# Layer 2 of a fused attention + two-MLP kernel as one Strassen level on 768-token superblocks

## Chip, cores and metric

One core of one Trainium2 chip. The time is the device time of the launch in microseconds (us), median of three runs. The core has five engines: TensorE (PE, with its weight loads shown as PEld), VectorE (DVE), ScalarE (ACT), GpSimd (POOL) and SyncE (SP, which issues the DMAs). TensorE multiplies a stationary 128x128 block of weights with a moving operand of up to 512 columns and adds the result into a bank of PSUM; all other data lies in SBUF.

## What is computed

```python
def _moe_ref(x, w_in, w_out):            # layer 1
    h = x @ w_in
    g = h * (1.0 / (1.0 + np.exp(-1.702 * h)))
    return (g @ w_out).astype(np.float32)

def _moe2_ref(x, w_in, w_out):           # layer 2
    h = x @ w_in
    r = np.maximum(h, 0.0)
    g = r * r
    return (g @ w_out).astype(np.float32)

# reference: x = attention(q, k, v) as 2304 tokens x 512; moe2(moe(x))
# w_in is 512 x 2048, w_out 2048 x 512, both arrive as float64
```

The attention is banded (32 keys, plain or dilated by 4), 4 batches x 8 heads x 576 x 64.

## The kernel before

Every product is made in three passes: an operand is split into a high part (a cast to fp32r) and a low part (value minus high part), and high x high, high x low and low x high are summed in PSUM.

Layer 1 goes over five blocks of tokens (512, 512, 256, 512, 512 columns, `BLOCKS1`, with the attention of later tokens worked in between), layer 2 over five more (`BLOCKS2`, the same sizes). `step` (L631) is one of the 16 slices f of 128 hidden features for one block: 12 matmuls "hidden" (four slices k of the inputs, three passes, L616 to L618) into a bank of PSUM named h, the activation (layer 1: `tanh` on ACT, L639, and `times_h` on DVE, L642; layer 2: `relu` on ACT, L649, and `square` on DVE, L652), the split of the result g into gh (`copy`, L251 on ACT or L253 on DVE) and gl (`minus`, L262, DVE), and 12 matmuls "project" (L683 to L685) into the four banks o, which sum over all 16 f. So a block is 16 x 24 = 384 matmuls of its number of columns. The last step of the last block is cut into two halves of 256 columns. The results go out through ost; layer 1's to a DRAM tensor x2d, from which layer 2 reads its input back.

All weights stay in SBUF: 32 places w{f}_{part} of 2 x 2 KB a partition. `weights` (L302) fills one: a load of the float64 words (L312), the top half word to f16 (`top`, ACT or DVE), `join` into a float32 (L327, DVE), high part, low part. Layer 2's weights go into the same places while layer 1's last block runs through them.

The order of the instructions on each engine is fixed beforehand by `Schedule.emit` (L132): tasks with costs, due times (`want`), predecessors and buffers are laid out one by one, and each engine then runs its list strictly in that order. SP does so too: a DMA that waits for a buffer holds up all DMAs behind it. `AHEAD` lets the hidden matmuls of a step run 24 matmuls (48 in layer 1's last block and in layer 2) ahead of their due time.

## Time and profile before

| | |
|---|---|
| median of 3 runs (lowest, highest) | 875.66 us (875.12, 877.23) |
| profiled execution: span, first to last instruction | 873.0 us |
| median over span (what lies around it) | 2.66 us |
| busy: PE, DVE, ACT, POOL | 863.3, 455.4, 368.1, 15.8 us |
| weight loads (PEld, beside PE) | 720.6 us |
| moved by DMA, mean rate | 64.99 MB, 74 GB/s |
| granted TensorE clock, mean | 1.000 |

No own time is given for the profiled execution beyond its span; the three runs lie 2.1 to 4.2 us above that span. Busy time is the time in which an engine has an instruction in work; matmuls overlap each other and their ends are modelled, so what one matmul costs is read from the distance of two starts, not from its duration.

### The profile page before, as it was taken

How to read it: one execution, taken by the hardware profiler on the slowest of the kernel's cores; microseconds unless marked ns; L12 is line 12 of the kernel's file. 1: busy time of each engine (PE TensorE's matmuls, PEld its weight loads, DVE VectorE, ACT ScalarE, POOL GpSimd, SP SyncE). 2: the span in 40 equal slices, each digit the busy share in tenths (PEclk: the TensorE clock that was granted, in tenths of full speed). 3: DMA queues.
4: the chain of work that ended last, by engine and by line, in shares of the span. 5: the costliest groups of instructions: out<-in, count | busy, mean ns of one | idle time of the engine just before them, and what ended most of it. 6: DMA issues, size and time to landing. Idle time of an engine off the chain costs nothing.

```text
span 873.0 us, 12807 instructions
## 1 busy us (share of the span) xinstructions
PE 863.3 (99%) x4758; PEld 720.6 (83%) x4758; DVE 455.4 (52%) x1254; ACT 368.1 (42%) x976; POOL 15.8 (2%) x25
## 2 busy tenths in 40 slices
PE   8999999999999999999999999999999999999997
PEld 6887778777899888888888888888889988888886
DVE  5998995466699843358788222322222232222222
ACT  7999995444455521134645222322222222222222
POOL 3300000000000000000000000000000000000000
PEclk9999999999999999999999999999999999999999
DMA  7655662111232020027554100100010000001001
GB/s 245 209 185 203 211 215 93 37 36 38 72 93 64 28 91 1 1 64 259 193 184 156 61 1 1 36 25 1 1 48 2 1 25 1 1 0 50 1 1 48
DMA packets 27534, 64.99 MB, mean 74 GB/s; under 512 B 3056, under 2 KB 9200, under 8 KB 27472
## 3 DMA queue, kind: packets, MB, share of 16 engines
q1 hardware_dynamic: 27472, 64.18, 22.1%
q8 instruction: 37, 0.61, 0.3%
q14 instruction: 25, 0.20, 0.1%
HBM read 54.73 MB, written 9.44 MB: 74 GB/s over the span
## 4 chain that ended last, share of the span: by engine, by line
PE 97%; ACT 1%; DVE 1%; DMA 0%; issue 0%; SPq 0%; DVEq 0%
PE h L616 16%; PE o L683 15%; PE h L618 15%; PE h L617 15%; PE o L684 15%; PE o L685 15%; PE s L467 3%; PE pv L568 2%; ACT sm L490 1%; DMA qk<-in_qkv 0%; PE tp L549 0%; PE warm L745 0%; DVE x L584 0%; ACT pt L251 0%; DVE pt L253 0%
## 5 line engine op out<-in xcount | busy, mean ns | idle before, releaser
L683 PE MATMUL o<-gh,wh 128*128 128x512 f32 (+3 forms) x648 | 238.5, 368 | 0.0
L685 PE MATMUL o<-gl,wh 128*128 128x512 f32 (+3 forms) x648 | 236.5, 365 | 0.0
L684 PE MATMUL o<-gh,wl 128*128 128x512 f32 (+3 forms) x648 | 236.5, 365 | 0.0
L616 PE MATMUL h<-x,wh 128*128 128x512 f32 (+3 forms) x520 | 190.9, 367 | 0.0
L618 PE MATMUL h<-x,wl 128*128 128x512 f32 (+3 forms) x520 | 187.3, 360 | 0.0
L617 PE MATMUL h<-x,wh 128*128 128x512 f32 (+3 forms) x520 | 187.1, 360 | 0.0
L262 DVE TENSOR_TENSOR gl<-g,gh 128x512 fp32r<-128x512 f32 (+3 forms) x163 | 102.1, 627 | 126.5 <-ACT gh L251 122.6
L683 PEld LDWEIGHTS o<-gh,wh 128*128 128x128 f32 x648 | 122.1, 188 | 21.6
L685 PEld LDWEIGHTS o<-gl,wh 128*128 128x128 f32 x648 | 122.2, 189 | 19.8
L684 PEld LDWEIGHTS o<-gh,wl 128*128 128x128 f32 x648 | 122.2, 189 | 19.3
L652 DVE TENSOR_TENSOR g<-g 128x512 f32<-128x512 f32 (+1 forms) x81 | 51.2, 632 | 157.9 <-ACT g L649 157.8
L251 ACT CAST gh<-g 128x512 fp32r<-128x512 f32 (+3 forms) x117 | 68.4, 585 | 133.8 <-PE o L684 126.1
L649 ACT ACTIVATE g<-h 128x512 f32<-128x512 f32 (+1 forms) x81 | 44.5, 550 | 165.4 <-PE h L618 165.4
L616 PEld LDWEIGHTS h<-x,wh 128*128 128x128 f32 x520 | 98.1, 189 | 17.9
L618 PEld LDWEIGHTS h<-x,wl 128*128 128x128 f32 x520 | 98.1, 189 | 15.1
L617 PEld LDWEIGHTS h<-x,wh 128*128 128x128 f32 x520 | 98.2, 189 | 14.0
L639 ACT ACTIVATE g<-h 128x512 f32<-128x512 f32 (+3 forms) x82 | 44.4, 543 | 112.6 <-PE h L618 112.1
L490 ACT ACTIVATE sm<-sm,st 96x128 f32<-96x128 f32 x180 | 70.4, 395 | 40.4 <-DVE st L483 40.3
L642 DVE SCALAR_TENSOR_TENSOR g<-g,h 128x512 f32<-128x512 f32 (+3 forms) x82 | 50.4, 616 | 67.5 <-ACT g L639 67.0
L534 DVE STREAM_TRANSPOSE pt<-sm 32x192 f32<-32x192 f32 x144 | 53.1, 369 | 5.4 <-ACT sm L257 3.5
L618 PE MATMUL h<-xx,wl 128*128 128x512 f32 (+1 forms) x132 | 50.5, 383 | 0.0
L617 PE MATMUL h<-xx,wh 128*128 128x512 f32 (+1 forms) x132 | 50.5, 383 | 0.0
(66 smaller groups left out, 695.6 us busy)
## 6 DMA issues: line engine op xcount, KB each, us to landing
raw<-in_w SPq DMA_DIRECT2D x64, 511.8 KB, 3.3
qk<-in_qkv SPq DMA_DIRECT2D x32, 304.0 KB, 3.0
v<-in_qkv SPq DMA_DIRECT2D x32, 192.0 KB, 2.5
x2d<-ost SPq DMA_DIRECT2D x16, 256.0 KB, 2.1
raw<-x2d SPq DMA_DIRECT2D x16, 256.0 KB, 2.8
out_T<-ost SPq DMA_DIRECT2D x14, 256.0 KB, 2.0
x2d<-ost SPq DMA_DIRECT2D x4, 128.0 KB, 1.7
raw<-x2d SPq DMA_DIRECT2D x4, 128.0 KB, 2.2
```

The costliest lines, as they stand in the source:

```text
L251: A.copy(out, in_)
L262: by_name[e].tensor_tensor(out=out, in0=a, in1=b, op=ALU.subtract)
L490: A.activation(out=m["sm", j][:, i], in_=m["sm", j][:, i], func=AF.Exp, bias=m["st"][:, 0, j, i:i + 1], scale=-1.0, accum_out=m["st"][:, 1 ...
L534: V.transpose(out=pt[32 * e:32 * e + 32, :, :, 32 * a:32 * a + 32].rearrange("p j i q -> p (j i) q"), in_=m["sm"][32 * a:32 * a + 32, :, : ...
L616: T.matmul(out, w_hi[:, ks], x[:, 0, k, a:z], start=(k == 0), stop=False)
L617: T.matmul(out, w_hi[:, ks], x[:, 1, k, a:z], start=False, stop=False)
L618: T.matmul(out, w_lo[:, ks], x[:, 0, k, a:z], start=False, stop=(k == KD - 1))
L642: V.scalar_tensor_tensor(out=g(), in0=g(), scalar=1.0, in1=h(), op0=ALU.add, op1=ALU.mult)
L652: by_name[e].tensor_tensor(out=g(), in0=g(), in1=g(), op=ALU.mult)
L683: T.matmul(out, w_hi[:, ds_], m["gh"], start=(f == 0 and a == 0 or extra), stop=False)
L684: T.matmul(out, w_lo[:, ds_], m["gh"], start=False, stop=False)
L685: T.matmul(out, w_hi[:, ds_], m["gl"], start=False, stop=(f == KF - 1))
```

## The change

Layer 2 is done on three superblocks of 768 tokens. Both products are cut 2 x 2 and made from seven products of quarters in place of eight (Winograd's form, `PRODUCTS`). A matmul has now 384 columns (`HN`).

- `prepare` makes the seven combinations of the weights for one pair of f slices, each as a high and a low part, from two loads; 16 such calls (8 of w_out, 8 of w_in) are due 10 us apart (`PREP`) from layer 1's block 3 on. Their results are written to DRAM, wo_s and wi_s; six of w_in also stay in the places wp1 to wp6.
- `stream` loads the combined weights back, two DMAs a place, for each superblock anew: 8 places of w_in and 7 of w_out.
- `x_prep` loads 768 tokens of x2d and makes and splits the seven combinations of the input.
- `hidden2` does the first product for one pair of f slices: seven products of 6 matmuls, with the sums of Winograd's form done by DVE and ACT from PSUM into the planes gq, then relu and square (two ACT instructions or one of DVE, on 768 elements), then the differences T1 and T3.
- `output2` does the second product: seven products of four chunks of 12 matmuls; every chunk's operand (768 elements) is split into gh and gl right before.

The 32 places of the weights become eight of 16 KB; they also hold the planes and the streamed weights. Outside of layer 2, one of three buffers for v is given up, and the masks are loaded by two DMAs.

```diff
-MORE_LATE = 1.0
-W2_GAP = 4.0
+GB_US = 340.0
+PREP = 10.0
...
-BLOCKS2 = [512, 512, 256, 512, 512]
+SB = 768
+HN = SB // 2
+NSB = NT // SB
+NPR = KF // 2
+A11, A12, A21, A22, S1, S2, S4 = range(7)
+S3 = A21
+PRODUCTS = (
+    (A11, "B11"), (S4, "B22"), (S1, "T1"), (S2, "T2"), (A12, "B21"), (S3, "T3"), (A22, "T4"),
+)
+PLANE = {"B11": 0, "B12": 1, "B21": 2, "B22": 3, "T1": 4, "T2": 3, "T3": 1, "T4": 2}
+G_SLOTS = (7, 2, 3, 4)
+S_SLOTS = (5, 6, 0, 1)
+LAG = 3
+KEPT = 6
+FIRST_SLOTS = (1, 2, 3, 4, 5, 6, 0, 1)
+X_EARLY = 20.0
...
     x2d = dram.tile([KD, P, NT], F32, name="x2d")
+    wi_s = dram.tile([NPR, P, 2 * 7 * 256], F32, name="wi_s")
+    wo_s = dram.tile([7, P, 2, NPR, 256], F32, name="wo_s")
...
-    for f in range(KF):
-        for part in range(2):
-            places[f"w{f}_{part}"] = 1
+    for j in range(NPR):
+        places[f"wp{j}"] = 1
...
+    def prepare(n, part, j, want, cls):
+        m = {}
+        odd = n % 2
+        raw_bs = [buffer("x1")] if odd else [buffer("raw"), buffer("raw")]
+        w_cls = ("rh", "rl") if cls == "r" else (cls, cls)
+        w_bs = [buffer("rh"), buffer("rl")] if cls == "r" else [buffer(cls)] * 2
+        gate = x_users["x1"] if odd else raws_free
...
+        joins = []
+        for i in range(2):
+            mi = {}
...
+            t = task(
+                "dma", moved(P * 4096), want - 10, lambda i=i: load_weights(raw(i), 1, 2 * j + i, part), gate, [raw_bs[i % len(raw_bs)]],
+                since=begin[3] - 12,
+            )
+            t = task(*TOP, want - 5, lambda e, i=i, mi=mi: raw_top(e, raw(i), mi), [t], [raw_bs[i % len(raw_bs)], c_b], True)
+            joins.append(task("dve", JOIN, want - 5, lambda i=i, mi=mi: raw_join(raw(i), mi), [t], [raw_bs[i % len(raw_bs)], c_b], True))
+        def combine(out, a, b, op):
+            V.tensor_tensor(out=at(out), in0=at(a), in1=at(b), op=op)
+        def combined(out, a, b, op, after):
+            return task("dve", pairs(256)[1][0], want - 4, lambda: combine(out, a, b, op), after, raw_bs, True)
+        t1 = combined(S1, A21, A22, ALU.add, joins)
+        t3 = combined(S3, A11, A21, ALU.subtract, [t1])
+        t2 = combined(S2, S1, A11, ALU.subtract, [t1])
+        t4 = combined(S4, A12, S2, ALU.subtract, [t2])
...
+        his, los = [], []
+        for i, odd_word, after in ((0, 0, [t3]), (1, 0, [t3]), (0, 1, [t2]), (1, 1, [t4])):
+            width = 256 if (i, odd_word) == (1, 1) else 512
...
+            hi = task(*copies(width), want - 2, high, after + slot_users[w_cls[0]], [raw_bs[i % len(raw_bs)], w_bs[0]], True)
+            los.append(task(*pairs(width), want - 2, low, [hi] + slot_users[w_cls[1]], [raw_bs[i % len(raw_bs)]] + w_bs[0:1 + (cls == "r")], True))
+            his.append(hi)
...
+        def store(hl):
+            src = wt(hl).bitcast(F32)
+            if part == 0:
+                nc.sync.dma_start(wi_s[j][:, hl * 1792:(hl + 1) * 1792], src.rearrange("p i c -> p (i c)"))
+            else:
+                nc.sync.dma_start(wo_s[:, :, hl, j].rearrange("i p c -> p i c"), src)
+        stores = [
+            task("dma", moved(P * 7168), want - 1, lambda hl=hl: store(hl), (his, los)[hl], [w_bs[hl]]) for hl in range(2)
+        ]
...
+    def stream(cls, want, src, shape, after):
...
+        def load(hl):
+            if "w" not in m:
+                m["w"] = slot(cls, shape, F32R, "ws")
+            nc.sync.dma_start(m["w"][:, hl].bitcast(F32).rearrange("p i c -> p (i c)"), src[:, hl * n:(hl + 1) * n])
+        ts = [
+            task("dma", moved(P * n * 4), want, lambda hl=hl: load(hl), after + slot_users[cls], [w_b]) for hl in range(2)
+        ]
+        return (lambda: m["w"]), w_b, ts
...
+    OPS = {"rh": ("B11",), "rl": ("B22",), "r": ("T1",), "x0": ("T2", "B21"), "x1": ("T3",), "raw": ("T4",)}
+    def x_prep(s, want, cls):
...
+        loads = [
+            task(
+                "dma", moved(P * SB * 4), want - 8,
+                lambda k=k: nc.sync.dma_start(stage()[:, k], x2d[k, :, c0:c0 + SB]),
+                [stored[i, k] for i in need] + slot_users[cls], [st_b],
+            )
+            for k in range(KD)
+        ]
...
+        def split(op, after):
+            b = bufs_of(op)
+            hi = task(*copies(n768), want, lambda e: copy(e, place(op, 0), quarter(op)), after + op_users[home[op][0]], [st_b, b[0]], True)
+            lo = task(*pairs(n768), want, lambda e: minus(e, place(op, 1), quarter(op), place(op, 0)), [hi], [st_b] + b, True)
...
+        split("B11", [loads[0], loads[1]])
+        split("B22", [loads[2], loads[3]])
+        t1 = combine("T1", "B12", "B11", done["B11"])
+        split("T1", [t1])
+        t3 = combine("T3", "B22", "B12", [t1] + loads[2:])
+        t2 = combine("T2", "B22", "T1", [t3] + done["B22"])
+        split("T2", [t2])
+        split("B21", [loads[2], loads[3]])
+        split("T3", [t3])
+        t4 = combine("T4", "B21", "T2", [t2] + done["B21"])
+        split("T4", [t4])
...
+    def hidden2(s, j, x, w, last, gate, planes):
...
+        def product(n, key, cls, first, bufs, after, lag):
+            a, op = PRODUCTS[n]
...
+                for k in range(2):
+                    ks = slice(k * P, (k + 1) * P)
+                    hi, lo = place(op, 0)[:, k], place(op, 1)[:, k]
+                    T.matmul(out, wt[:, 0, a, ks], hi, start=(first and k == 0), stop=False, skip_group_check=True)
+                    T.matmul(out, wt[:, 0, a, ks], lo, start=False, stop=False, skip_group_check=True)
+                    T.matmul(out, wt[:, 1, a, ks], hi, start=False, stop=(k == 1), skip_group_check=True)
+            return task("pe", 6 * mm(HN), at + (n + lag) * unit, run, w_ready + x_done2[op] + after, bufs + [w_b] + bufs_of(op))
...
+        p_1 = product(0, "X", "s", True, [x_b], last, 0)
+        p_3 = product(1, "Y3", "o", True, [y3], [p_1], 0)
+        p_5 = product(2, "Z", "h", True, [z_b], [p_3], 0)
+        e1 = kept("p1", "X", [p_1] + gate, [x_b, p1_b], when(-LAG))
+        e3 = kept("p3", "Y3", [p_3], [y3, p3_b], when(1 - LAG))
+        p_6 = product(3, "X", "s", False, [x_b], [p_5, e1], LAG)
+        u2 = summed(None, "p3", "X", [p_6, e3], [x_b, p3_b], when(3))
+        c12 = summed(1, "p3", "Z", [p_5, u2], [z_b, p3_b, g_b], when(4))
+        p_2 = product(4, "Y2", "o", True, [y2], [p_6], LAG)
+        c11 = summed(0, "p1", "Y2", [p_2, e1], [y2, p1_b, g_b], when(4))
+        p_7 = product(5, "X", "s", False, [x_b], [p_2, u2], LAG)
+        e7 = kept("u3", "X", [p_7], [x_b, u3_b], when(5))
+        c22 = summed(3, "u3", "Z", [p_5, e7], [z_b, u3_b, g_b], when(6))
+        p_4 = product(6, "Y4", "o", True, [y4], [p_7], LAG)
+        c21 = summed(2, "u3", "Y4", [p_4, e7], [y4, u3_b, g_b], when(6))
...
+        ways = ("act", "dve"), (2 * (0.19 + n768 / 1536), pairs(n768)[1][0])
...
+            t1 = task(*pairs(n768), when(12), lambda e: diff(4, 1, 0), [a01, b01], [g_b], True)
+            t3 = task(*pairs(n768), when(13), lambda e: diff(1, 3, 1), [t1, a23, b23], [g_b], True)
...
+    def output2(s, planes, next_slot):
...
+        for n, (a, op) in enumerate(PRODUCTS):
+            want = at + n * LB
+            cls = next_slot()
+            wt, w_b, loaded = stream(cls, want - 30, wo_s[a].rearrange("p h j c -> p (h j c)"), [P, 2, NPR, 256], wo_stored)
...
+            for q in range(NPR // 2):
...
+                def high(e, mm_=mm_, third=third, pl=pl, plane=plane):
+                    pool, tag, k = (wst, "raw", RAW_BUFS) if third else (gpool, "gh", 2)
+                    mm_["h"] = pool.tile([P, 2, HN], F32R, tag=tag, bufs=k, name="gh")
+                    copy(e, mm_["h"], pl["tile"]()[:, plane])
+                def low(e, mm_=mm_, pl=pl, plane=plane):
+                    mm_["l"] = gpool.tile([P, 2, HN], F32R, tag="gl", name="gl")
+                    minus(e, mm_["l"], pl["tile"]()[:, plane], mm_["h"])
+                hi = task(*copies(n768), wq - 3, high, pl[op] + (raws_free if third else []) + split_last[0:1], [pl["b"], gh_b], True)
+                lo = task(*pairs(n768), wq - 3, low, [hi] + split_last[1:2], [pl["b"], gh_b, gl_b], True)
+                split_last[:] = [hi, lo]
+                if op == "B22":
+                    pl["T2"] = [task(*pairs(n768), wq + LB, lambda e, pl=pl: pl["diff"](3, 3, 4), [hi, lo] + pl["T1"] + pl["T3"], [pl["b"]], True)]
...
+                def project(q=q, mm_=mm_, wt=wt, key=key, first=first, b_cls=b_cls):
+                    w = wt()
+                    for d in range(2):
+                        if first and q == 0:
+                            m[key, d] = bank(b_cls, key)
+                        out, ds_ = m[key, d][:, 0:HN], slice(d * P, (d + 1) * P)
+                        for jj in range(2):
+                            j = 2 * q + jj
+                            hi, lo = mm_["h"][:, jj], mm_["l"][:, jj]
+                            T.matmul(out, w[:, 0, j, ds_], hi, start=(first and j == 0), stop=False, skip_group_check=True)
+                            T.matmul(out, w[:, 1, j, ds_], hi, start=False, stop=False, skip_group_check=True)
+                            T.matmul(out, w[:, 0, j, ds_], lo, start=False, stop=(j == NPR - 1), skip_group_check=True)
+                t = task("pe", LB / 4, wq, project, loaded + [hi, lo] + bank_after.get(n, []) + before, bs + [w_b, gh_b, gl_b])
...
+    want, n = begin[3], 0
+    for part, j in [(1, j) for j in range(NPR)] + [(0, j) for j in range(KEPT, NPR)]:
+        prepare(n, part, j, want, "r")
+        want, n = want + PREP, n + 1
+    r_stores = wo_stored + [t for ts in wi_stored.values() for t in ts]
+    first_w = {}
+    for j in range(KEPT):
+        first_w[j] = prepare(n, 0, j, max(want, begin[4] + (2 * j + 6) * step_len(512)), f"wp{j + 1}")
+        want, n = want + PREP, n + 1
...
+    x = x_prep(0, T2 - X_EARLY, "wp0")
...
+    for s in range(NSB):
+        planes, last = {}, []
...
+                w = stream(cls, T2 + s * LSB + j * LA - 30, wi_s[j], [P, 2, 7, 256], wi_stored[j])
+            last, by_op = hidden2(s, j, x, w, last, all_prepared if s == 0 else [], planes)
+            slot_users[cls] = list(by_op.values())
+        op_users = {cls: [by_op[op] for op in ops] for cls, ops in OPS.items()}
+        op_users["rh"] = op_users["rl"] = op_users["r"] = op_users["rh"] + op_users["rl"] + op_users["r"]
+        if s + 1 < NSB:
+            x = x_prep(s + 1, T2 + s * LSB + NPR * LA + 2 * LB, "x2")
+        output2(s, planes, next_slot)
...
```

In the order of instructions three places show what moves. First VectorE in layer 1's block 3 (g, gh, gl: a step's activation and split; raw, c: weights in the making; wt: a combination's high or low part), before:

```order
L642 SCALAR_TENSOR_TENSOR g<-g,h 128x512
L253 CAST gh<-g 128x512
L262 TENSOR_TENSOR gl<-g,gh 128x512
L262 TENSOR_TENSOR xx<-raw_3774,xx 128x512
L642 SCALAR_TENSOR_TENSOR g<-g,h 128x512
```

and with the change:

```order
L338 SCALAR_TENSOR_TENSOR raw<-raw,c 128x512
L277 TENSOR_TENSOR wt<-raw,wt 128x2x256 x2
L277 TENSOR_TENSOR wt<-raw,wt 128x512
L277 TENSOR_TENSOR wt<-raw,wt 128x256
L680 SCALAR_TENSOR_TENSOR g<-g,h 128x512
L338 SCALAR_TENSOR_TENSOR raw<-raw,c 128x512
L887 TENSOR_TENSOR raw<-raw 128x256
L277 TENSOR_TENSOR gl<-g,gh 128x512
L887 TENSOR_TENSOR raw<-raw 128x256 x2
L268 CAST wt<-raw 128x2x256
```

Between a step's g and its gl there now stand instructions of the weights. Second VectorE in layer 2, in the second product of the first superblock (gq: planes and their differences; p: sums of the output; X, Z: PSUM):

```order
L1136 TENSOR_TENSOR gq<-gq 128x768
L277 TENSOR_TENSOR gl<-gq,gh 128x768
L1170 TENSOR_TENSOR p_5770<-p_5770,X 128x384
L1170 TENSOR_TENSOR p_5775<-p_5775,X 128x384
L1170 TENSOR_TENSOR p_5770<-p_5770,Z 128x384
L1170 TENSOR_TENSOR p_5775<-p_5775,Z 128x384
L277 TENSOR_TENSOR gl<-gq,gh 128x768
```

One gl stands there for every chunk of TensorE, with differences and sums between. Third SyncE over the end of the first superblock and the start of the second (ws: streamed weights; xs: input):

```order
L958 DMA ws<-wo_s 128x2048 x12
L988 DMA xs<-x2d 128x768 x4
L958 DMA ws<-wo_s 128x2048 x2
L958 DMA ws<-wi_s 128x1792 x2
L1176 DMA out_T<-p_5770 128x384
L1176 DMA out_T<-p_5775 128x384
```

Before, layer 2's part of this queue held the loads of x2d and the stores of the result alone.

## Rows read from the trace of the kernel before

**Rows 1.** The page, busy time: engine, us, share, instructions
```profile
PE 863.3 (99%) x4758; PEld 720.6 (83%) x4758; DVE 455.4 (52%) x1254; ACT 368.1 (42%) x976; POOL 15.8 (2%) x25
```
**Rows 2.** The page, 40 slices: PE, and the granted clock in tenths
```profile
PE   8999999999999999999999999999999999999997
...
PEclk9999999999999999999999999999999999999999
```
**Rows 3.** The page, the chain of work that ended last, by engine
```profile
PE 97%; ACT 1%; DVE 1%; DMA 0%; issue 0%; SPq 0%; DVEq 0%
```
**Rows 4.** Timeline of PE, layer 2, 512 columns: start us, us
```profile
600.04 0.39 PE L617 MATMUL h<-x,wh 128*128 128x512 f32 x1
...
603.89 0.39 PE L616 MATMUL h<-x,wh 128*128 128x512 f32 x1
```
**Rows 5.** Timeline of PE, layer 2, 256 columns
```profile
654.75 0.28 PE L684 MATMUL o<-gh,wl 128*128 128x256 f32 x1
...
659.91 0.28 PE L618 MATMUL h<-x,wl 128*128 128x256 f32 x1
```
**Rows 6.** Instructions that read wl, weight loads: ns min/median/max
```profile
L618 PEld LDWEIGHTS h<-x,wl x520: 187/188/192, 30.2 to 772.0; 128*128 128x128 f32 x174
```
**Rows 7.** Stretches: length, busy PE, PEld, DVE, ACT, POOL, clock, DMA share, GB/s
```profile
390.00:412.00 22.00, 22.00 (x99) 18.18 (x98) 18.84 (x35) 11.95 (x20) 0.00 (x0) 1.00 0.77 253
...
455.00:477.00 22.00, 22.00 (x99) 18.22 (x98) 19.83 (x35) 12.29 (x22) 0.00 (x0) 1.00 0.46 157
```
**Rows 8.** Groups by line and form, DVE: count, busy us, mean ns
```profile
L262 DVE TENSOR_TENSOR gl<-g,gh 128x512 fp32r<-128x512 f32 x125 | 86.1, 689 | 112.3 <-ACT gh L251 109.7 <-PE pv L568 0.7
...
L327 DVE SCALAR_TENSOR_TENSOR raw<-raw,c 128x512 uint32<-128x512 uint32 x64 | 43.5, 686 | 2.1 <-ACT c L251 1.8
...
L262 DVE TENSOR_TENSOR gl<-g,gh 128x256 fp32r<-128x256 f32 x34 | 14.4, 423 | 14.2 <-ACT gh L251 12.9 <-PE o L684 0.7
L253 DVE CAST gh<-g 128x512 fp32r<-128x512 f32 x28 | 12.0, 427 | 7.0 <-PE o L684 5.1
```
**Rows 9.** Timeline of DVE, layer 1's last block: start us, us
```profile
440.67 0.43 DVE L253 CAST gh<-g 128x512 fp32r<-128x512 f32 x1
441.01 0.68 DVE L262 TENSOR_TENSOR wl<-raw,wh 128x512 fp32r<-128x512 f32 x1
441.61 0.69 DVE L262 TENSOR_TENSOR gl<-g,gh 128x512 fp32r<-128x512 f32 x1
442.22 0.68 DVE L327 SCALAR_TENSOR_TENSOR raw<-raw,c 128x512 uint32<-128x512 uint32 x1
```
**Rows 10.** Groups by line and form, ACT
```profile
L251 ACT CAST gh<-g 128x512 fp32r<-128x512 f32 x97 | 60.3, 622 | 120.3 <-PE o L684 112.6 <-DVE g L642 3.8 <-DVE g L652 2.1
...
L251 ACT CAST gh<-g 128x256 fp32r<-128x256 f32 x16 | 6.5, 407 | 13.5 <-PE o L684 13.4
```
**Rows 11.** Stretch of the loads of layer 2's weights, columns as in rows 7
```profile
395.00:400.00 5.00, 5.00 (x24) 4.14 (x23) 4.79 (x11) 1.40 (x3) 0.00 (x0) 1.00 0.98 330
```
**Rows 12.** The page, DMA issues: count, KB each, median us to landing
```profile
raw<-in_w SPq DMA_DIRECT2D x64, 511.8 KB, 3.3
...
x2d<-ost SPq DMA_DIRECT2D x16, 256.0 KB, 2.1
...
x2d<-ost SPq DMA_DIRECT2D x4, 128.0 KB, 1.7
```
**Rows 13.** Instructions on x2d, SP: ns min/median/max of one DMA issue
```profile
L714 SPq DMA_DIRECT2D x2d<-ost x20: 320/327/431, 138.9 to 481.2; - x20
```
**Rows 14.** Timeline of the end
```profile
866.09 0.28 PE L685 MATMUL o<-gl,wh 128*128 128x256 f32 x1
...
866.41 0.69 DVE L259 TENSOR_SCALAR raw<-o 128x512 f32<-128x512 f32 x1 [0.43 <-PE o L685]
...
867.89 0.28 PE L685 MATMUL more<-gl,wh 128*128 128x256 f32 x1
...
869.30 0.91 SPq L714 DMA_DIRECT2D out_T<-raw  x2
```

More of the change, by code (lines that the diff above doesn't have):

```diff
@@ L289, in attention_mlp_mlp @@
     split_task = {}
-    wbuf = {}
+    wp_tile = {}
+    wp_buf = [buffer(f"wp{j}") for j in range(NPR)]
+    wp_last = [[] for _ in range(NPR)]
     chain = {}
-    tops = [wst.tile([P, DM], U32, tag=f"c{i}", name="c") for i in range(C_BUFS)]
-    top_count = [0]
+    x_users = {"x0": [], "x1": [], "x2": []}
+    tops = [wst.tile([P, DM], U32, tag="c", bufs=C_BUFS, name="c") for _ in range(C_BUFS)]
+    free_tops = list(tops)
     def zero_tops():
@@ L300, in attention_mlp_mlp, with as_words, load_weights, raw_top @@
     tops_zero = [task("pool", 1.2, -1000, zero_tops)]
-    def weights(layer, f, part, want):
+    raws_free = []
+    def as_words(t):
+        return t.rearrange("p n t -> p (n t)")
+    def load_weights(raw, layer, f, part):
+        nc.sync.dma_start(as_words(raw).bitcast(U16)[:, 0:4 * DM - 1], (w1, w2)[layer][f, part].bitcast(U16)[:, 1:4 * DM])
+    def raw_top(e, raw, m):
+        m["c"] = free_tops.pop(0)
+        halves = as_words(raw).bitcast(BF16).rearrange("p (n t) -> p n t", t=4)[:, :, 2]
+        copy(e, m["c"].bitcast(F16).rearrange("p (n t) -> p n t", t=2)[:, :, 1], halves)
@@ L305, in weights, with raw_join @@
+    def raw_join(raw, m):
+        V.scalar_tensor_tensor(
+            out=raw[:, :, 0], in0=raw[:, :, 0], scalar=13, in1=m["c"],
+            op0=ALU.logical_shift_right, op1=ALU.bitwise_or,
+        )
+        free_tops.append(m["c"])
+    TOP = ("act", "dve"), (0.67, 0.38)
+    JOIN = 0.602
+    def weights(f, part, want):
         m = {}
-        raw_b, c_b, w_b = buffer("raw"), buffer("c"), buffer(f"w{f}_{part}")
-        name = f"{f}_{part}"
+        raw_b, c_b, w_b = buffer("raw"), buffer("c"), wp_buf[f // 2]
@@ L335, in high_part @@
         def high_part(e):
-            wh[layer, f, part] = wpool.tile([P, DM], F32R, tag="wh" + name, name="wh" + name)
-            copy(e, wh[layer, f, part], value())
+            places_of()
+            copy(e, wh[f, part], value())
         def low_part(e):
-            wl[layer, f, part] = wpool.tile([P, DM], F32R, tag="wl" + name, name="wl" + name)
-            minus(e, wl[layer, f, part], value(), wh[layer, f, part])
-        t = task("dma", 1.456, want - LEAD[0], load, (), [raw_b], since=RAW_FROM, late=MORE_LATE * layer)
@@ L592, in attention_mlp_mlp, with step @@
     close = {}
-    def step(layer, blk, f, want, a=0, z=None, own=False):
+    def step(blk, f, want, a=0, z=None):
         z = z or blk["n"]
@@ L600, in step @@
         m = {}
-        late = layer or blk["i"] == len(BLOCKS1) - 1
+        late = blk["i"] == len(BLOCKS1) - 1
         h_cls = "s" if f % 2 and late else "h"
@@ L605, in step @@
         x_b = blk["buf"]
-        w_in, w_out = wbuf[layer, f, 0], wbuf[layer, f, 1]
+        w_b = wp_buf[f // 2]
         t = None
@@ L668, in step, with project @@
             blk["o_buf"] = [buffer("o") for _ in range(KD)]
-            blk["o"], blk["ost_buf"], blk["evacs"] = {}, {}, {}
+            blk["o"], blk["evacs"] = {}, {}
         for d in range(KD):
-            extra = own
-            more_b = [buffer("sshh"[d])] if extra else []
-            def project(d=d, extra=extra):
+            def project(d=d):
                 if f == 0 and a == 0:
                     blk["o"][d] = bank("o", "o")
-                w_hi, w_lo = wh[layer, f, 1], wl[layer, f, 1]
-                if extra:
-                    m["more", d] = bank("sshh"[d], "more")[:, 0:n]
-                out, ds_ = m["more", d] if extra else blk["o"][d][:, a:z], slice(d * P, (d + 1) * P)
-                T.matmul(out, w_hi[:, ds_], m["gh"], start=(f == 0 and a == 0 or extra), stop=False)
+                w_hi, w_lo = wh[f, 1], wl[f, 1]
+                out, ds_ = blk["o"][d][:, a:z], slice(d * P, (d + 1) * P)
+                T.matmul(out, w_hi[:, ds_], m["gh"], start=(f == 0 and a == 0), stop=False)
                 T.matmul(out, w_lo[:, ds_], m["gh"], start=False, stop=False)
@@ L790, in attention_mlp_mlp @@
     l0 = (begin[1] - begin[0]) / KF
-    for f, part in order(0):
-        weights(0, f, part, begin[0] + l0 * (f + (0, 1.5)[part]))
+    for f, part in order():
+        weights(f, part, begin[0] + l0 * (f + (0, 1.5)[part]))
     blocks = []
```

407 lines of the change are left out of this document (291 added, 116 removed).

## Prediction

> **What bounds the kernel now.** I read the page's busy times first [rows 1]: TensorE is at work in 863.3 of 873.0 us, VectorE and ScalarE in about half. The slices [rows 2] show that this holds from the second slice to the last but one, at the full granted clock of 2.4 GHz, and the chain of work that ended last [rows 3] is TensorE's for 97%. So before the change nothing but the number and the price of matmuls sets the time of layer 2, and a stall anywhere in it would be new.
>
> The price comes from the distance of starts, not from durations. With 512 columns, 17 distances take 603.89 - 600.04 = 3.85 us, 0.2265 us each [rows 4]; with 256 columns, 43 distances take 5.16 us, 0.1200 us each [rows 5]. The weight loads beside them last 0.188 us whatever the columns [rows 6], longer than a 256-column distance, so they overlap one another and do not set it. No row has 384 columns; between the two prices the middle is 0.1733 us. I take it as exact: both neighbours lie on one line, columns at 2.4 GHz plus 13 ns.
>
> **Removed and added on TensorE.** Layer 2 before: five blocks of 384 matmuls, of which 1512 have 512 columns and 432 have 256 (the block of 256, and the last step in halves, 48 for 24). 1512 x 0.2265 + 432 x 0.1200 = 342.5 + 51.8 = 394.3 us. After: per superblock 8 pairs x 7 products x 6 matmuls and 7 products x 4 chunks x 12, that is 336 + 336; three times, 2016 of 384 columns: 2016 x 0.1733 = 349.3 us. The change takes 45.0 us from the engine that bounds. The columns fall by one eighth, 110,592 or 46.1 us at 2.4 GHz; 72 matmuls more give 1 us back.
>
> **What must stay hidden.** Five things are new beside it.
>
> *Making the weights, in layer 1's blocks 3 and 4.* These blocks are 32 steps x 24 x 0.2265 = 174 us; the first of the 16 calls of `prepare` starts some 10 us before, so 184 us are there. VectorE has in them, counted from the new order: 176 instructions of 512 elements (64 joins, 48 low parts, 32 products and 32 gl of the steps), 80 of 256, 11 of 768 for the input of the first superblock, some 35 casts and 3 copies of results. Durations are 0.687 us for 512, 0.423 for 256, 0.427 for a cast [rows 8]; 768 elements, one more step of 0.264, come to 0.951. But they overlap too: one starts 0.605 us after the other, a cast takes 0.34 [rows 9]. By distances the list takes 176 x 0.605 + 80 x 0.34 + 11 x 0.87 + 35 x 0.34 + 3 x 0.605 = 157 us, 85% of 184; by durations 182 us, 99%. The stretch in which the kernel before makes layer 2's weights is as full, 18.84 of 22 and 19.83 of 22 us, with TensorE busy in all of it [rows 7]. So I take a loss of 1.5 us, between 0 and 3 plus what a wait in VectorE's fixed list costs: gl stands there behind low parts of the weights that wait for a store to free their buffer. If that cover goes, gl is late, then the project matmuls.
>
> *The stores of the combined weights.* The 16 calls load 16.8 MB and store 29.4 MB; with x2d it is 52 MB in 184 us, 281 GB/s. The engines moved 330 GB/s at a share of 0.98 [rows 11]: 85% of that. One call is 2.88 MB, 8.7 us at 330, and is due every 10 us or more. A store of 0.92 MB should land after 1.3 + 2.8 = 4.1 us: 128 KB take 1.7 us and 256 KB 2.1 [rows 12], so the first 1.3 us are fixed. Its rows in wo_s are seven pieces of 1 KB a partition; the 128 KB stores [rows 12] had such rows too and lie on the same line, so I add nothing. The issue is less sure: all DMAs of the trace with 128 rows take SP 0.33 us [rows 13], one with 896 pieces between 0.33 and 7 x 0.33 = 2.3 us. I take the low end, since the time is the same from the shortest row to the longest, and keep the high end as a rival. The seven pieces of a partition lie 2 MiB apart in DRAM, which no DMA of this trace does. The Trainium skill, page "DMA: Bandwidth & Descriptors", section "Latency and other measured facts", says that copies whose rows lie 2 MiB apart ran at 164 in place of 214 GB/s; by that rule the 14.7 MB of wo_s would take an estimated 13 us more, and the sum, if none of it hid, would be 848 us.
>
> *Streaming, in layer 2.* 77.1 MB of weights (18 places of w_in, 24 less the six kept, at 1.84, and 21 of w_out at 2.10), 1.6 of input and 4.7 of results: 83.4 MB in 349.3 us, 239 GB/s; in the second and third superblock 32.5 MB per 116.4 us, 279 GB/s. Again 85% of 330 [rows 11]. Four places go round, a product uses one for 7 to 8 us and a load takes 5.6 to 6.4 us, so a load may be three products late before anyone waits. SP's list holds the result's stores among these loads, but they wait for sums that are a few us old. I cost it at nothing.
>
> *Operands of the products.* VectorE has 185 instructions of 768 elements, 168 of 384 and 3 casts in layer 2: 185 x 0.951 + 168 x 0.556 + 2 = 271 us, 78% of 349.3; ScalarE 129 of 768 at 0.622 + 0.215 = 0.837 and 72 of 384 at 0.515 [rows 10], 145 us. Tightest is the second product: gl has two buffers, so the low part of chunk k+2 starts when chunk k is done. From there to the matmul that reads it are 2.08 + 0.35 = 2.43 us; a reader starts 0.04 us after a matmul's end [rows 14], so 0.04 + 0.95 + 0.04 = 1.03 us are needed. 1.4 us are left for what stands between two low parts, 0.93 us a chunk on average. In the first product every sum has two other products, 2.1 us or more, between its matmuls and the next ones in its bank, against about 1 us for one sum or copy. I take 0.3 us of waiting at each of the five changes between first and second product, 1.5 us, bounds 0 and 8.
>
> *From layer 1 to layer 2, start and end.* The last call of `prepare` can write into wp6 only after layer 1's step 13, 5 us before the end; four low parts, a cast, a copy and two low parts of the input follow on VectorE, done about 1 us after layer 2's first matmul, and the first matmul that needs them comes ten products, 10 us, later. 1 us, bounds 0 and 3. The third buffer of v and the second DMA of the masks touch the first 24 us: 0, bounds 0 and 1. The end (5.1 us from the last matmul to the end of the span [rows 14]) stays within half a us.
>
> **Sum.** The profiled execution has a span of 873.0 us, and 2.66 us lie between it and the median. 873.0 - 45.0 + 1.5 + 1.5 + 1.0 = 832.0 us of span, **834.7 us** as a median. Its own range is 829 (no wait at all, the end a little shorter) to 841.
>
> **Rivals.**
> - *The weights come late.* With 2.3 us for the issue of a 896-piece store, two of them a call, the eight calls of w_out take 4 us more each; 1.3 us of a call's 10 are spare, so 8 x 2.7 = 22 us, less the 10 us of lead, 12 us: **847 us** (842 to 853). TensorE would then wait in block 3, where gl stands behind a weight's low part, or in one piece at the start of layer 2. Against it: 1 KB rows show no surcharge [rows 12].
> - *The stores to wo_s move slowly,* because of where their pieces lie; no row bounds it. At three quarters of 330 GB/s the two stores of a call take 1.9 us more, 0.6 above the spare 1.3: 8 x 0.6 = 5 us, inside the lead. At half the rate they take 5.6 us more: 8 x 4.3 = 34 us less 10, **859 us**. The Trainium skill's page "DMA: Bandwidth & Descriptors", named above, speaks for the first of the two rates.
> - *Operands come late in layer 2.* There are 168 + 84 = 252 groups of matmuls, each handed operands by VectorE or ScalarE in a fixed order. 0.1 us of waiting at each is 25 us: **860 us** (854 to 872). For it: by durations VectorE is at 90% in the second product. Against it: the slack of 1.4 us above.
> - *The stream sets the pace, slower than before.* Layer 2 would have to last 394.3 + 2.6 us: 83.4 MB in 397 us, a rate under 210 GB/s. At 200 GB/s it lasts 417 us: **898 us**. For it: the longest stretch shown at a high rate is 22 us at 253 GB/s [rows 7]; 350 us of it are not shown. Against it: that stretch had a share of 0.77, the same 330 at full work.
> - *The change does not do what it says*, because 384 columns cost more than the line gives. With the weight load's 0.188 us [rows 6] as a floor, layer 2 would take 379 us, the median 864; the 256-column distance of 0.120 us [rows 5] rules it out.
>
> **How the numbers follow.** Forecast 0.65; late weights by the issue 0.15; slow stores 0.04; late operands 0.09; slower by the stream 0.05; within 0.3% (873 to 878 us, about what the measurement can tell from no change) 0.02, from a mixture of late weights and operands. Faster by more: 0.65 + 0.15 + 0.04 + 0.09 = 0.93. The range reaches from 829, no wait at all, to 853, the end of late weights; it leaves out slow stores, late operands, no change and the slower side, 0.20.
>
> **What would show it.** Right: 384-column starts 0.173 us apart in layer 2, TensorE idle there for under 5 us, layer 2 about 352 us long, DMA at 240 to 280 GB/s through it, the granted clock at full speed throughout. Late weights: waits of TensorE for gl in blocks 3 and 4, or one gap before the first 384-column matmul; SP issues of wo_s of over 1 us. Late operands: many short gaps before the matmuls that read gl, released by VectorE. A stream too slow: gaps released by the DMAs of ws. Wrong altogether: a distance well off 0.173, or a lower granted clock.

## The result and the profile after

The changed kernel takes **834.92 us** (median of four runs, 834.27 to 838.11), the kernel before 875.39 (874.93 to 877.23): a ratio of 0.954, interval 0.952 to 0.956. The prediction was 834.7, range 829 to 853. The profiled execution has a span of 832.5 us. The times of the experiments are medians of four executions too, except experiment 6, where one disturbed execution of 2504.62 us is left out.

The page, busy time and the chain of work that ended last, answer to [rows 1, 3]:

```profile
PE 819.7 (98%) x4830; PEld 734.9 (88%) x4830; DVE 636.6 (76%) x1521; ACT 418.3 (50%) x1024; POOL 15.8 (2%) x25
...
PE 94%; DMA 4%; DVE 1%; ACT 1%; issue 0%; SPq 0%; ACTq 0%
```

TensorE still sets the end, but the chain now holds 4% of DMA, 30.7 us, where it held 4.3 us. Of these, 17.8 us are three loads before 143 us; the other 12.9 us are two stores at the change of layers. The waits of TensorE show what that costs (engine, line, what it waited for, us in total, times, longest):

```profile
PE s L504 <- DMA qk<-in_qkv: 3.6, 3, 1.7
PE X L1077 <- DVE p L1095: 3.0, 1, 3.0
```

The first is at the start of the kernel and was there before (2.5 us). The second, 10 us after the beginning of layer 2, is the only wait of layer 2 but one of 0.2 us. The timeline around it:

```profile
484.38 0.34 PE L1079 MATMUL Y<-xo,wt 128*128 128x384 f32 x1
...
486.63 1.09 ACT L266 COPY p<-Y 128x384 f32<-128x384 f32 x2 [7.46 <-DMA x2d<-ost]
487.14 1.16 DVE L1095 TENSOR_TENSOR p<-p,X 128x384 f32<-128x384 f32 x2 [1.83 <-ACT p L266]
...
487.75 0.50 PE L1077 MATMUL X<-xo,wt 128*128 128x384 f32 x1 [3.03 <-DVE p L1095]
488.05 0.52 PE L1078 MATMUL X<-xo,wt 128*128 128x384 f32 x1
...
491.25 0.41 PE L1079 MATMUL Y<-xo,wt 128*128 128x384 f32 x1
491.50 0.34 PE L1077 MATMUL X<-xo,wt 128*128 128x384 f32 x1
```

Read it from the bottom up. Matmuls are 0.32 us apart from 488.05 to 491.25 where they are 0.173 elsewhere: half clock, 1.2 in place of 2.4 GHz (the mean of 485 to 500 us, shown under experiment 2, is 0.89). Before that TensorE stood for 3.03 us for a sum of VectorE, VectorE for a copy of ScalarE, and ScalarE had stood 7.46 us for a *store* to x2d: a result of layer 1, not a weight of layer 2. The chain shows how long those stores took to land (start, us, what):

```profile
472.29 0.61 ACT ost L272
...
472.91 5.05 DMA x2d<-ost
...
478.05 0.61 ACT ost L272
...
478.68 7.86 DMA x2d<-ost
...
486.63 0.49 ACT p L266
```

And SP's timeline what lay ahead of them:

```profile
470.22 2.52 SPq L932 DMA_DIRECT2D wi_s<-wt  x2
472.91 1.88 SPq L726 DMA_DIRECT2D x2d<-ost  x2
475.42 1.65 SPq L958 DMA_DIRECT2D ws<-wi_s  x2
478.68 0.84 SPq L726 DMA_DIRECT2D x2d<-ost  x2
```

Layer 1's last block has four results and two buffers of the tag ost. The first two were stored behind two stores of 0.9 MB, and the first of them landed after 5.05 us. The third and fourth result had to wait for these buffers and were stored behind two loads of 0.9 MB; the third landed after 7.86 us. p3, the copy of the product p_3 that layer 2 keeps for its sums, has its buffer in the same tag, so its first copy came after all that.

Blocks 3 and 4 and layer 2 otherwise, by stretches (columns as in [rows 7]), and the DMAs' landing (columns as in [rows 12]):

```profile
405.00:425.00 20.00, 20.00 (x90) 16.57 (x89) 15.30 (x26) 9.97 (x16) 0.00 (x0) 1.00 0.92 344
...
590.00:648.00 58.00, 58.00 (x336) 58.00 (x335) 38.70 (x59) 16.11 (x30) 0.00 (x0) 1.00 0.72 261
```

```profile
wo_s<-wt SPq DMA_DIRECT2D x16, 896.0 KB, 6.6
wi_s<-wt SPq DMA_DIRECT2D x16, 896.0 KB, 5.7
...
x2d<-ost SPq DMA_DIRECT2D x16, 256.0 KB, 4.9
```

With the DMA engines at a share of 0.92 and 344 GB/s TensorE is busy in all of 20 us, and it has no wait from 290 to 474 us, so the making and storing of the weights is hidden. But a 256 KB store that landed in 2.1 us before [rows 12] now takes 4.9 (both medians).

### The profile page after: what moved, and what is told of

It is laid out like the page before. It is cut to its first block, busy times and chain, and to the rows that moved or that the text cites. A ratio compares the mean times of both kernels' runs of the same rounds, so it can differ in the third digit from the quotient of the medians.

```text
span 832.5 us, 13335 instructions
## 1 busy us (share of the span) xinstructions
PE 819.7 (98%) x4830; PEld 734.9 (88%) x4830; DVE 636.6 (76%) x1521; ACT 418.3 (50%) x1024; POOL 15.8 (2%) x25
## 4 chain that ended last, share of the span: by engine, by line
PE 94%; DMA 4%; DVE 1%; ACT 1%; issue 0%; SPq 0%; ACTq 0%
PE h L653 8%; PE o L705 8%; PE h L655 8%; PE h L654 8%; PE o L707 8%; PE o L706 8%; PE Y L1226 3%; PE X L1226 3%; PE Y L1225 3%; PE X L1225 3%; PE Y L1224 3%; PE X L1224 3%; PE X L1077 3%; PE s L504 3%; PE X L1078 3%; PE X L1079 3%
## 5 line engine op out<-in xcount | busy, mean ns | idle before, releaser
L653 PE MATMUL h<-x,wp 128*128 128x512 f32 (+3 forms) x328 | 122.9, 375 | 0.0
L705 PE MATMUL o<-gh,wp 128*128 128x512 f32 (+3 forms) x328 | 121.4, 370 | 0.4 <-ACT ost L272 0.4
L655 PE MATMUL h<-x,wp 128*128 128x512 f32 (+3 forms) x328 | 119.4, 364 | 0.0
L707 PE MATMUL o<-gl,wp 128*128 128x512 f32 (+3 forms) x328 | 119.4, 364 | 0.0
L654 PE MATMUL h<-x,wp 128*128 128x512 f32 (+3 forms) x328 | 119.2, 363 | 0.0
L706 PE MATMUL o<-gh,wp 128*128 128x512 f32 (+3 forms) x328 | 119.1, 363 | 0.0
L266 ACT CAST gh<-gq 128x768 fp32r<-128x768 f32 x83 | 68.6, 838 | 79.0 <-PE X L1225 32.9
L277 DVE TENSOR_TENSOR gl<-gq,gh 128x768 fp32r<-128x768 f32 x84 | 80.3, 956 | 34.4 <-PE X L1226 21.5
L653 PEld LDWEIGHTS h<-x,wp 128*128 128x128 f32 x328 | 61.8, 188 | 12.9
L705 PEld LDWEIGHTS o<-gh,wp 128*128 128x128 f32 x328 | 61.8, 188 | 12.7 <-ACT ost L272 0.8
L707 PEld LDWEIGHTS o<-gl,wp 128*128 128x128 f32 x328 | 61.8, 188 | 10.1 <-DVE gl L277 0.3
L655 PEld LDWEIGHTS h<-x,wp 128*128 128x128 f32 x328 | 61.8, 188 | 10.0
L706 PEld LDWEIGHTS o<-gh,wp 128*128 128x128 f32 x328 | 61.9, 189 | 9.5
L654 PEld LDWEIGHTS h<-x,wp 128*128 128x128 f32 x328 | 61.9, 189 | 9.1
L277 DVE TENSOR_TENSOR gl<-g,gh 128x512 fp32r<-128x512 f32 (+3 forms) x82 | 50.9, 621 | 5.5 <-ACT gh L266 4.1
L266 ACT CAST c<-raw 128x512 f16<-128x512 bf16 x58 | 44.7, 776 | 18.9 <-DMA raw<-in_w 17.3
```

The source lines that it names most:

```text
L266: A.copy(out, in_)
L277: by_name[e].tensor_tensor(out=out, in0=a, in1=b, op=ALU.subtract)
L653: T.matmul(out, w_hi[:, ks], x[:, 0, k, a:z], start=(k == 0), stop=False)
L654: T.matmul(out, w_hi[:, ks], x[:, 1, k, a:z], start=False, stop=False)
L655: T.matmul(out, w_lo[:, ks], x[:, 0, k, a:z], start=False, stop=(k == KD - 1))
L705: T.matmul(out, w_hi[:, ds_], m["gh"], start=(f == 0 and a == 0), stop=False)
```

## Experiments

**1. The stores ahead of the loads.** The loads of the seventh and eighth weight of layer 2 are made to come after layer 1's last result stores.

```diff
- w = stream(cls, ..., wi_s[j], [P, 2, 7, 256], wi_stored[j])
+ w = stream(cls, ..., wi_s[j], [P, 2, 7, 256], wi_stored[j] + ([stored[4, d] for d in range(KD)] if s == 0 else []))
```

> Edit: the loads of the seventh and eighth weight of layer 2 (ws<-wi_s) stand on SP behind all four result stores of layer 1's last block instead of between them. Theory (shared buffer): the wait of 3.03 us before p_7 at 484.72 us, and the half clock that follows it until 491.25 (11 matmuls 0.32 us apart instead of 0.173, some 1.7 us), come from the copy p<-Y, whose buffer is one of the two of the tag ost and is freed only when the last x2d store lands, 7.86 us after its issue because four 0.9 MB loads are ahead of it in the DMA engines. With the stores ahead they land in about 3 us, by 482; the copy needs to start by 483.6. Wait 0, clock at full speed from 475 on, span 832.5 - 3.0 - 1.7 = 827.8 us, median about 830.2. Rival (fixed order of VectorE and ScalarE): the copy is late because of what stands ahead of it on its engine; then over 2 us of the wait stay and the median stays above 833. Rival (clock apart from the wait): the wait goes but the clock still falls at the change of layers; median about 831.9.

Measured: 830.08 us (829.39 to 831.37), ratio 0.948 (0.946 to 0.950), span 828.4. TensorE has no wait before p_7, the product where it had stood for 3.03 us, and the clock stays at 1.0. SP's timeline and ScalarE's:

```profile
473.74 6.56 SPq L726 DMA_DIRECT2D x2d<-ost  x4
...
478.73 1.23 ACT L272 ACTIVATE ost<-o 128x512 f32<-128x512 f32 x2 [2.02 <-DMA x2d<-ost]
...
480.39 8.06 SPq L958 DMA_DIRECT2D ws<-wi_s  x4
...
481.48 0.48 ACT L266 COPY p<-Y 128x384 f32<-128x384 f32 x1 [1.52 <-PE X L1079]
```

The copy that waited until 486.63 starts at 481.48, and nobody waits for it. Wait and half clock went together; both rivals fall. The third result still waits 2.02 us for the first store, which costs nothing here. (The expectation counts four loads ahead of the last stores; the changed kernel's timeline of SP shows two.)

**2. Places of their own for the results.** The four results go to the slot x2, which is free by then; p3 shares nothing with them. (Since no result waits for another's store any more, all four stores also come ahead of the loads in SP's list.)

```diff
- out = opool.tile([P, 512], F32, tag="ost", name="ost")
+ if last_blk:
...
+     blk["osts"] = slot("x2", [P, KD, 512], F32, "osts")
+     out = blk["osts"][:, d]
+ else:
+     out = opool.tile([P, 512], F32, tag="ost", name="ost")
```

> Edit: the four results of layer 1's last block get four places of their own (in the slot of x2, which is free by then), so that p3 of layer 2 shares no buffer with them. Theory (shared buffer): no wait before p_7, full clock, and ScalarE does not wait 2.18 us for a store between the results either; median about 830.2 (829.6 to 830.8), the same as with the stores first, and the x2d stores may land as late as they like. Rival (the DMA queue itself, through something other than this buffer, e.g. weights or input behind the stores): this edit leaves 2 us or more of wait, and only the order of the stores helps.

Measured: **829.85 us** (828.84 to 830.07), ratio 0.947 (0.946 to 0.949), span 828.0: the same as the first, by the other of the two means, but as the four stores also come earlier, this run does not show the shared buffer alone; the next one does. The stretch after the change of layers has its matmuls and its clock back, though the DMA engines are at a share of 1.01 just before. The first line is of the changed kernel, the others of version 2:

```profile
485.00:500.00 15.00, 12.25 (x61) 12.25 (x62) 10.59 (x19) 7.67 (x11) 0.00 (x0) 0.89 0.37 132
...
474.00:485.00 11.00, 11.00 (x65) 10.88 (x64) 5.73 (x10) 3.61 (x8) 0.00 (x0) 1.00 1.01 378
485.00:500.00 15.00, 15.00 (x88) 15.00 (x87) 11.21 (x17) 3.52 (x7) 0.00 (x0) 1.00 0.48 194
```

This version 2 beats both kernels, by 5.1 us the changed one. Most of the other experiments are made on it, so that this wait does not mix in.

**3. Places of their own, and two stores late again,** on version 2: the stores of the third and fourth result are put behind the loads of the seventh weight, and in SP's list they then stand behind all four loads of the seventh and eighth.

```diff
+ if s == 0 and j == 6:
+     for t in w[2]:
+         for d in (2, 3):
+             t["next"].append(stored[len(BLOCKS1) - 1, d])
+             stored[len(BLOCKS1) - 1, d]["left"] += 1
  last, by_op = hidden2(s, j, x, w, last, ...)
```

> Edit, made on the kernel whose last results of layer 1 have places of their own (829.85 us): the third and fourth result's stores are put behind all four loads of the seventh and eighth weight of layer 2 in SP's list, so that they are late again, later than in the changed kernel, but p3 still shares no buffer with them. Theory (a late store costs time only through the buffer that it holds): no wait before p_7, full clock, 829.9 us (829 to 831), though these stores land at 487 us or later. Rival (late stores cost time by themselves, through a full queue or through the second superblock's input, which reads x2d): a wait of 2 us or more in layer 2, 833 us or more.

Measured: 829.92 us (829.13 to 830.60), ratio 0.948 (0.947 to 0.950). SP's timeline:

```profile
476.62 9.08 SPq L968 DMA_DIRECT2D ws<-wi_s  x4
485.79 1.03 SPq L736 DMA_DIRECT2D x2d<-osts  x2
```

The two stores go out at 485.79 us, 7 us later than in the changed kernel, and TensorE has no wait in layer 2 but 0.2 us for gl. So here a late store costs nothing by itself; it costs through the buffer that it keeps.

**4. Pieces not 2 MiB apart.**

```diff
- wo_s = dram.tile([7, P, 2, NPR, 256], F32, name="wo_s")
+ wo_s = dram.tile([7, P + 1, 2, NPR, 256], F32, name="wo_s")[:, 0:P]
```

> Edit: one row of 16 KB more between the seven pieces of wo_s, so that the pieces of a partition lie 2 MiB + 16 KB apart in DRAM instead of 2 MiB. Theory (the address does not matter): a store of wo_s still lands after about 6.6 us (6.2 to 7.0), SP's issue stays near 0.43 us, time unchanged, 834.9 within 0.8. Rival (stores with rows 2 MiB apart move slowly): the landing falls to that of wi_s, 5.7 us or less, and the DMA share of blocks 3 and 4 falls from about 0.90 to 0.85; the time still changes by less than 1 us since TensorE does not wait there.

Measured: the median landing is 6.7 us, against 6.6; so the distance of 2 MiB is not what makes these stores slower than wi_s's (what does was not settled), and the Trainium skill's rule on rows 2 MiB apart (page "DMA: Bandwidth & Descriptors", section "Latency and other measured facts"), which is told of copies, does not show in these stores. The time was not the same, though: 833.22 us (832.68 to 833.86), ratio 0.951 (0.950 to 0.953). The timeline tells why:

```profile
488.26 0.45 PE L1077 MATMUL X<-xo,wt 128*128 128x384 f32 x1 [2.47 <-DVE p L1095]
488.54 0.34 PE L1078 MATMUL X<-xo,wt 128*128 128x384 f32 x1
488.72 0.35 PE L1079 MATMUL X<-xo,wt 128*128 128x384 f32 x1
```

The same wait is 2.47 us instead of 3.03, and the clock does not fall after it: 0.18 us from start to start. In layer 2 that is 0.56 us of wait and 1.67 us of half clock (12 distances taking 3.75 us in place of 2.08). The wait is shorter because layer 2 begins 1.07 us later (475.20 us), while the third result's store lands only 0.51 us later (487.04): the difference is the 0.56. Nothing ties that to the address; the beginning of layer 2 lies between 473.95 and 475.41 us in the other runs (experiment 9 aside) too. In three of the four executions the mean clock is 1.000, in one 0.998 as in all four of the changed kernel; that it fell after this wait there too is likely, but not shown.

**5. A quarter more traffic in layer 2,** on the changed kernel.

```diff
  nc.sync.dma_start(m["w"][:, hl]..., src[:, hl * n:(hl + 1) * n])
+ spare = dram.tile([P, n // 4], F32, name=f"spare{len(spares)}")
+ nc.sync.dma_start(spare, src[:, hl * n:hl * n + n // 4])
```

> Edit: behind each streamed load of layer 2 another DMA copies a quarter as much from the same weights to a place in DRAM that nobody reads: 25% more traffic, 77 to 96 MB, and 78 more issues on SP. Theory (the stream is hidden with room): the DMA share of the second and third superblock rises from 0.72 to about 0.90, rate from 265 to about 330 GB/s, TensorE waits under 3 us more: 835 to 838. Rival (the room is not there: loads are already as late as they may be): every product waits a few tenths of a us, 845 or more. Rival (a copy within DRAM costs the engines twice its bytes): 1.5 times the traffic, share at 1.0, and the second and third superblock last 0.72 x 1.5 = 1.08 of now, 9 us more each: about 853.

Measured: 838.08 us (837.62 to 839.01), ratio 0.957 (0.956 to 0.959). In the stretch 590 to 648 us the share rose from 0.72 to 0.86. The profiled execution is the longest of the four, its span 837.2 us, 4.7 more than that of the changed kernel: layer 2 begins 1.28 us later, the wait at the change of layers is 3.9 in place of 3.0, and two waits for gl take 1.8; the rest, 0.7, was not settled. No wait for a streamed weight shows: the stream is hidden with a quarter to spare. Both rivals fall: no product waits a few tenths of a us, and a copy within DRAM does not take twice its bytes here, which would have put the share at 1.0.

**6. Half as much again,** on version 2, with `n // 2`.

> Edit, made on the kernel whose last results of layer 1 have places of their own (829.85 us): behind each streamed load of layer 2 another DMA copies half as much from the same weights to a place in DRAM that nobody reads, 77 to 116 MB. With a quarter more, the DMA share of the five stretches of 58 to 63 us rose from 0.81, 0.72, 0.75, 0.72, 0.52 to 0.97, 0.86, 0.93, 0.85, 0.71. Theory (a stream that the engines carry until they are full): twice that rise gives 1.13, 1.00, 1.11, 0.98, 0.90, so that two stretches grow by 0.13 x 58 + 0.11 x 58 = 14 us, the rest is hidden: 844 us (840 to 850). Rival (the loads' order on SP: any lateness of one load delays all behind it, the result stores too): waits in every product, 855 or more. Rival (what the quarter cost, 3 us, was only the longer wait at the change of layers and a few stores): under 834.

Measured: 838.27, 839.70 and 841.28 us, ratio 0.959 (0.957 to 0.961): some 10 us, less than the 14 of a full queue and just under its 840. It is neither spread evenly nor a wait for weights. VectorE, TensorE, then a stretch:

```profile
588.59 1.05 DVE L1186 TENSOR_TENSOR q<-u,Z 128x384 f32<-128x384 f32 x2 [4.52 <-DMA out_T<-p]
...
590.56 0.44 PE L1242 MATMUL Y<-gl,ws 128*128 128x384 f32 x1 [3.51 <-DVE gl L277]
...
592.00:594.00 2.00, 2.00 (x8) 2.00 (x8) 0.00 (x0) 0.00 (x0) 0.00 (x0) 0.50 0.96 385
```

A sum waits for the buffer of an earlier result whose store (out_T<-p) was issued behind big loads and copies; gl stands behind the sum on VectorE; TensorE waits, and the clock halves. It happens twice, 3.51 and 2.25 us, together 5.8 us of wait, and the mean clock of 0.995 over 838 us takes 4.2 more: together the 9.9 by which the span grew. So the first thing to break under more traffic is a small store again, not the stream, and the second rival is right in its mechanism, not in its size.

**7 and 8. More work on VectorE in the second product,** on version 2: half of each low part made twice, then all of it.

```diff
  minus(e, mm_["l"], pl["tile"]()[:, plane], mm_["h"])
+ minus(e, mm_["l"][:, 0], pl["tile"]()[:, plane, 0], mm_["h"][:, 0])
```

> Edit, made on the kernel whose last results have places of their own (829.85 us): VectorE makes the first half of each chunk's low part (gl) twice, 84 instructions of 384 elements more, about 0.47 us each by distance and 0.556 by duration. Theory (VectorE's rate, hidden with little room): in the second product of the first superblock VectorE is busy 46.5 of 58 us, 1.66 us a chunk of 2.08; with the addition 2.13 to 2.22, so 0.05 to 0.14 us a chunk is not hidden: 84 x that = 4 to 12 us, 834 to 842. Rival (operands already come just in time): all of it is paid, 84 x 0.47 = 39 us, 869. Rival (much room): within 1 us of 829.9.

> Edit, made on the kernel whose last results have places of their own (829.85 us): VectorE makes each chunk's whole low part (gl) twice, 84 instructions of 768 elements more, about 0.87 us each by distance and 0.956 by duration. Theory (VectorE's rate): 2.53 to 2.62 us a chunk against 2.08, so 0.45 to 0.54 us a chunk is paid: 38 to 45 us, 868 to 875. Rival (operands already come just in time): 84 x 0.87 = 73 us, 903. Rival (much room): under 840.

Measured: 847.68 us (847.58 to 847.81), ratio 0.968 (0.967 to 0.970), with half; 871.45 (870.87 to 871.78), ratio 0.995 (0.994 to 0.997), with all: 17.8 and 41.6 us. The second came within its 38 to 45, the first went past its 12. With half, the waits of the weight loads in layer 2:

```profile
PEld Y L1237 <- DVE gl L277: 8.8, 18, 1.2
PEld Z L1237 <- DVE gl L277: 7.0, 9, 1.2
...
PEld X L1237 <- DVE gl L277: 4.2, 14, 0.4
```

41 waits, 20.0 us, though VectorE's mean was to fit nearly. Its timeline in version 2 shows why a mean does not do (first line: a chunk with nothing else; then a chunk with four sums of the output, and two with a difference each):

```profile
560.08 0.96 DVE L277 TENSOR_TENSOR gl<-gq,gh 128x768 fp32r<-128x768 f32 x1 [1.12 <-PE X L1236]
...
567.21 1.01 DVE L1180 TENSOR_TENSOR p<-p,X 128x384 f32<-128x384 f32 x2
568.14 1.01 DVE L1180 TENSOR_TENSOR p<-p,Z 128x384 f32<-128x384 f32 x2
569.07 0.95 DVE L277 TENSOR_TENSOR gl<-gq,gh 128x768 fp32r<-128x768 f32 x1
569.94 0.95 DVE L1146 TENSOR_TENSOR gq<-gq 128x768 f32<-128x768 f32 x1
570.81 0.95 DVE L277 TENSOR_TENSOR gl<-gq,gh 128x768 fp32r<-128x768 f32 x1
571.68 0.95 DVE L1146 TENSOR_TENSOR gq<-gq 128x768 f32<-128x768 f32 x1
```

A plain chunk leaves VectorE 1.12 us idle; one with a difference of planes (L1146) takes 2 x 0.87 = 1.74 of the chunk's 2.08 and leaves 0.34. The one with four sums takes 569.94 - 567.21 = 2.73, more than 2.08; the two buffers of gl let it pass without a wait. With half more low part a pair takes 2.33:

```profile
559.26 0.95 DVE L1146 TENSOR_TENSOR gq<-gq 128x768 f32<-128x768 f32 x1
560.13 1.54 DVE L277 TENSOR_TENSOR gl<-gq,gh 128x768 fp32r<-128x768 f32 x2
561.59 0.95 DVE L1146 TENSOR_TENSOR gq<-gq 128x768 f32<-128x768 f32 x1
```

561.59 - 559.26 = 2.33, over 2.08. The waits fit this: from 532 to 565 us, where differences or the next superblock's input stand in nearly every chunk, nine waits are 0.27 to 0.37 us long, and two, in chunks with two such instructions, 1.14 and 1.16. The idle time of plain chunks elsewhere does not help these, since with two buffers of gl it cannot be saved up. Operands do not come just in time (39 and 73 us were not paid), but the cover is 0.34 us in a chunk with one companion and nothing of its own in one with two.

**9. Each store to wo_s twice,** on version 2.

```diff
  nc.sync.dma_start(wo_s[:, :, hl, j].rearrange("i p c -> p i c"), src)
+ nc.sync.dma_start(wo_t[:, :, hl, j].rearrange("i p c -> p i c"), src)
```

> Edit, made on the kernel whose last results have places of their own (829.85 us): each store of combined weights to wo_s is followed by the same store to a second place that nobody reads: 16 stores of 0.92 MB more between 310 and 390 us, 14.7 MB. There the DMA engines move 288 GB/s at a share of 0.89, 324 at full work. Theory (the stores are hidden, but with little cover): a call of 2.88 MB becomes 4.72 MB and takes 14.6 us instead of the 10 in which it is due, 8 calls are 37 us late, and some 10 us of lead and the emptier stretch behind them (0.61 to 0.74 from 410 us on) take a part: 845 to 860. TensorE then waits in block 3 for gl, which stands on VectorE behind low parts of the weights. Rival (nothing in layer 1 waits for the stores within tens of us): under 833. Rival (SP's issue of 896 pieces is what a store costs): 16 x 0.43 = 7 us, 837.

Measured: 857.21 us (856.43 to 858.59), ratio 0.979 (0.977 to 0.981): 27.4 us, in the theory's range. VectorE's waits from 320 to 440 us, then the landings:

```profile
DVE wt L278 <- DMA wo_t<-wt: 15.0, 7, 3.0
DVE wt L269 <- DMA wo_t<-wt: 14.9, 8, 2.5
```

```profile
wo_s<-wt SPq DMA_DIRECT2D x16, 896.0 KB, 8.8
wo_t<-wt SPq DMA_DIRECT2D x16, 896.0 KB, 10.5
```

In version 2 the same stretch has 1.5 us of such waits for wo_s and 0.9 for wi_s. VectorE's list is fixed, so what stands behind a weight's part on it is late too, gl and gh and g, and TensorE waits 17.5 us for these three; the mean clock of 0.989 over 855.7 us takes some 9.4 more.

## Why the prediction was right, term by term

What was right is the mechanism: the matmuls of layer 2 at 0.173 us each set the gain, and the making, storing and streaming of the weights stays hidden. That the sum of spans, 832.0, came out at 832.5 is luck: the change of layers cost 3.9 us more than its term, and the weights, the operands and the end together 3.5 less.

- *Matmuls: right.* The distance is 0.173 us: from the matmul at 475.19 to that at 484.38 are 53 distances, 9.19 / 53. Version 2 has its first matmul of layer 2 at 474.52 and its last start at 824.39 us, 2015 distances of 0.1736, 349.9 us; 349.3 were predicted. So the line through 256 and 512 columns holds at 384.
- *Making the weights, 1.5 us: 0.3.* No wait of TensorE in blocks 3 and 4; layer 2 begins at 474.13 us, where before 867.89 + 0.12 - 394.3 = 473.71, and 0.1 of the difference is there from the start. VectorE is busy in 152.5 of the 184 us from 290 to 474, near the 157 reckoned by distances and not the 182 by durations. What covers it is thin all the same (experiment 9).
- *Stores at nothing: right, for two reasons of unequal worth.* One issue of 896 pieces takes SP 0.43 us (0.376 to 1.591), not 2.3, so the rival of late weights loses its price. The landing, estimated at 4.1 us, is 6.6; that it still hides is due to the 10 us between calls.
- *Streaming at nothing: right,* 261 GB/s at a share of 0.72; a quarter more would still have hidden nearly all.
- *Operands, 1.5 us: at most 0.7,* all that 2015 distances of version 2 lose against 0.1733. The mean of 0.93 us a chunk hid that some chunks have 0.34 us left or, with two companions, nothing of their own (experiment 7).
- *From layer 1 to layer 2, 1.0 us, bounds 0 and 3: 4.9.* This is the step that failed. The text asked when the last weights and the input would be ready, which they were, and not who else used the buffers of layer 2's first temporaries. p3 shares its tag with layer 1's results, whose stores, at 2.1 us in the trace of before, took 5.05 and 7.86 us behind transfers of 0.9 MB. The first matmul after the wait came 487.75 - 484.55 = 3.20 us late, and 1.67 us of half clock followed; no term stood for that. Experiments 1 to 3 give back 4.8 to 5.1 us.
- *The end, within half a us: 1.5 us shorter.* From the last matmul's start to the end of the span 832.5 - 828.87 = 3.63 us, against 5.11 [rows 14]. Of the last two stores the first is issued beside the last matmul, and both issues are over 828.79 + 1.38 - 828.87 = 1.30 us after its start; before, the last two were issued from 869.30 on, 1.41 us after the last matmul's start, and over after 2.32 [rows 14].

```profile
828.79 1.38 SPq L1176 DMA_DIRECT2D out_T<-u  x2
828.87 0.34 PE L1226 MATMUL Y<-gl,ws 128*128 128x384 f32 x1
```

873.0 - 45.0 + 0.1 (start) + 0.3 + 4.9 + 0.7 - 1.5 = 832.5. The forecast's own low end, 829, is about where version 2 lies. One of the signs by which the prediction would be "wrong altogether" did appear, a lower granted clock, for 3.75 us; it came with the wait that no term stood for, and not from the price of a matmul, which held.
